# A fused attention and MLP kernel: another sequence for the same 883 operations

## The chip, the core and the metric

The kernel runs on one core of a Trainium2 chip. The core has engines that work side by side, each on its own queue and in order: PE (matrix products; PEld is its loading of weights), DVE and ACT and POOL (elementwise work), and SP, which here only issues DMAs. The metric is the device time in microseconds (us) of one execution. The profile is of one execution that the hardware profiler recorded.

## The reference, cut to what matters

```python
# S = 2048 rows, D = 448, F = 1792, 16 heads of 28; window of 8 keys, 2 apart
def A(x, wqkv, wo):                       # x is layernorm(input)
    q, k, v = split(x @ wqkv)             # 16 heads each
    idx = pos[:, None] - 2 * arange(8)    # below 0: masked
    attn = softmax(q . k[idx] * Dh ** -0.5)
    return (attn . v[idx]) @ wo
def B(x, w1, w2, w3, w4):                 # x is layernorm(h)
    g = gelu(layernorm(x) @ w1)           # four groups of 112 columns
    hs = [g0 down 1, g1 up 1, g2 down 2, g3 up 2] @ w2   # rows shifted, by group
    x1 = x + hs
    return x1 + gelu(layernorm(x1) @ w3) @ w4
h   = x + A(layernorm(x), wqkv, wo)
out = h + B(layernorm(h), w1, w2, w3, w4)
```

All inputs are bfloat16.

## The kernel before

**Tiles and stages.** The 2048 rows are 16 row tiles of 128. The first half of the work goes in four blocks of four row tiles (t = 0 to 3): N1 (first layernorm), A1 (q and k), V, A2 (logits and exp), A3 (attention times v, then wo and the residual), B1 (layernorm, w1, gelu). The second half goes in five units of 2, 4, 4, 4 and 2 row tiles (u = 0 to 4): B2 (w2 with the shifted groups, residual, statistics), T (layernorm and transposition), W3 (w3 and gelu) and B3 (w4, residual, output). Below, "W33" is stage W3 of unit 3, "T0" stage T of unit 0, and so on. Names of buffers: `lntm` holds normalized rows, `actT` the same transposed, `vt` and `vw` the values before and after they are laid out per window by DMAs, `bd_r` the attention weights spread into blocks by DVE (one of 16 products with the mask `bmask` each), `ht` the shifted rows of g that a DMA brings, `h3T` the gelu of w3's product, `qk_r` products and, at the end, output rows. `w3`, `w4`, and the two parts of w2 (`w2_s`, `w2_l`; `w_s` and `w_l` in the profile) are loaded by DMAs in pieces: w3 in two halves of 896 KB, w4 in two of 784 KB, `w2_l` in eight or so small pieces. The profile calls all of them `in_B_w_dram`, and their places in the arena `arena`.

**Rows turned.** A transposition of 128-column chunks is done by PE (matrix product with `ident`) or by a DMA (`DMA_TRANSPOSE actT<-lntm`), by block: `TURN` gives t or d for each.

**What sets the order.** The stages above are functions that only record operations, 883 in all, each with its engine, its instructions and the operations that it must follow. A table of numbers, `ORDER`, then lists all 883 in one sequence, and a second one, `OTHER`, names the operations that run on their second engine (an eviction of PE's results by DVE and not by ACT, or the other way round). `_Sched.arrange` walks through the sequence once and deals it out. Each engine gets its own operations in that order. Buffers (8 PSUM banks, 4 of `actT`, 2 of `bd_r`, 16 of `h3T` and so on) go to whoever comes next in the sequence, the longest free one first, and the new owner waits for the old one's last user. And DMA transpositions and plain DMAs of SP never overlap, as this piece of `arrange` (L207 to L212) says:

```python
            if op.insts[0][0] == "dma_start_transpose":
                op.deps.update(turned + moved)
                turned, moved = [op], []
            elif op.is_dma and not callable(op.chan):
                op.deps.update(turned)
                moved.append(op)
```

A transposition waits until every plain DMA listed since the last one has landed (`moved`), and plain DMAs wait until it has landed (`turned`); the stores of outputs, whose channel is a function, are free of both. So the place of a load in the table decides what the next transposition waits for.

All operations are emitted by one helper, so that the profile has nearly every instruction on line L1013 (waits that stand alone on L1011, ACT's table loads on L1008), and names of tiles tell the groups apart.

Of the kernel before, what the change touches and what calls it, by code (L numbers as in the profile page):

```python
# [17 lines left out]
RESIDUAL = 'ttvv'  # L18
DENSE = 2
ORDER = """  # L20
# [31 lines left out]
"""  # L52
OTHER = """
97 99 186 189 238 350 484 493 496 550 556
"""
FULL = (4,)
FILL = (0, 0, 0, 0)
# [997 lines left out]
```

## Time and profile before

| | |
|---|---|
| three runs | 191.86, 193.0, 195.99 us (median 193.0) |
| the profiled execution | 191.67 us, its span 190.0 us |
| granted TensorE clock, mean | 1.000 |
| PE busy | 181.8 us, 96% of the span, 2528 matmuls |
| DVE / ACT / POOL busy | 125.7 / 122.8 / 27.8 us |
| DMA queue q1 | 18.23 MB, 40.6% of 16 engines' span |

Busy shares are means over the span. The first 80 us hold the attention blocks, in which PE, DVE and ACT are all nearly always busy; after that DVE and ACT are busy a third to two thirds of the time and PE goes on.

### The profile page before, as it was taken

The numbers are of one execution on the slowest core, as the hardware profiler recorded it, in microseconds if no ns is written. First come the engines' busy times: TensorE is split into PE (matmuls) and PEld (weight loads), VectorE is DVE, ScalarE is ACT, GpSimd is POOL, SyncE is SP. The second block draws the span as 40 slices with busy tenths as digits, with TensorE's granted clock in tenths as the row PEclk, the third lists the DMA queues.
The fourth block names the chain that finished last, engine by engine and source line by source line (L and its number), as shares of the span: only waits on it lengthen the run. The fifth ranks groups of instructions, "written<-read, shape, count | busy, mean of one in ns | idle before, by whom it ended". The sixth has DMA issues, their size and how long they took to land.

```text
span 190.0 us, 5846 instructions
## 1 busy us (share of the span) xinstructions
PE 181.8 (96%) x2528; PEld 96.0 (51%) x2528; DVE 125.7 (66%) x220; ACT 122.8 (65%) x287; POOL 27.8 (15%) x67
## 2 busy tenths in 40 slices
PE   6999999998999999699999989999999999999994
PEld 2575335364534655475545534554445544455673
DVE  6989999999999899995378248823095357000503
ACT  3469999988999899675966878732715006630340
POOL 2380000000000000422260000060003507200000
PEclk9999999999999999999999999999999999999999
DMA  5990656853306599805033110571110600800401
GB/s 151 352 255 26 159 110 164 227 131 75 90 8 128 111 298 249 192 5 110 16 31 86 53 33 0 114 114 38 45 26 2 138 1 24 131 0 3 146 26 48
DMA packets 33634, 18.60 MB, mean 98 GB/s; under 512 B 21208, under 2 KB 33096, under 8 KB 33608
## 3 DMA queue, kind: packets, MB, share of 16 engines
q1 hardware_dynamic: 33608, 18.23, 40.6%
q8 instruction: 20, 0.33, 0.7%
q14 instruction: 6, 0.05, 0.1%
HBM read 8.14 MB, written 1.84 MB: 53 GB/s over the span
## 4 chain that ended last, share of the span: by engine, by line
PE 83%; DVE 5%; ACT 4%; DMA 3%; SPq 1%; issue 1%; POOL 1%; POOLq 0%; DVEq 0%
PE ps L1013 83%; ACT arena L1013 2%; DMA actT<-lntm 2%; SPq L1013 1%; DVE lntm L1013 1%; DVE arena L1013 1%; DMA w_l<-in_B_w_dram 1%; ACT actT L1013 1%; DVE st L1013 1%; DVE bd_r L1013 1%; DVE qk_r L1013 1%; POOL rs_y L1013 0%; ACT lntm L1013 0%; POOL ident L1013 0%; ACT h3T L1013 0%
## 5 line engine op out<-in xcount | busy, mean ns | idle before, releaser
L1013 PE MATMUL ps<-actT,arena 64*128 64x512 bf16 (+2 forms) x812 | 70.2, 325 | 2.4 <-DVE arena L1013 1.6
L1013 ACT ACTIVATE h3T<-ps 128x512 bf16<-128x512 f32 (+1 forms) x70 | 31.8, 513 | 41.5 <-PE ps L1013 41.0
L1013 PEld LDWEIGHTS ps<-actT,arena 64*128 64x128 bf16 (+1 forms) x812 | 35.6, 96 | 31.5 <-issue 3.4
L1013 PE MATMUL ps<-arena,h3T 64*128 64x448 bf16 (+3 forms) x434 | 44.3, 343 | 0.0
L1013 ACT ACTIVATE arena<-ps 128x512 bf16<-128x512 f32 (+6 forms) x67 | 30.8, 505 | 6.7 <-PE ps L1013 5.8
L1013 PEld LDWEIGHTS ps<-arena,h3T 64*128 64x128 bf16 (+1 forms) x434 | 22.6, 94 | 19.7 <-ACT h3T L1013 0.5
L1013 DVE TENSOR_TENSOR qk_r<-arena 128x4096 bf16<-128x4096 bf16 (+1 forms) x16 | 32.0, 2013 | 0.0
L1013 DVE SCALAR_TENSOR_TENSOR qk_r<-ps,mrs,arena 128x448 bf16<-128x448 f32 (+2 forms) x17 | 10.6, 652 | 30.2 <-PE ps L1013 30.2
L1013 POOL TENSOR_TENSOR arena<-arena,xin 128x448 f32<-128x448 f32 x16 | 16.5, 1056 | 78.6 <-ACT lntm L1013 61.6
L1013 DVE TENSOR_TENSOR bd_r<-arena,bmask 80x2048 bf16<-80x2048 bf16 x16 | 19.1, 1216 | 2.9 <-ACT arena L1013 2.9
L1013 DVE SCALAR_TENSOR_TENSOR arena<-xin,rs_y,ps 128x448 f32<-128x448 bf16 x16 | 10.4, 670 | 12.0 <-PE ps L1013 12.0
L1013 PE MATMUL ps<-wo_s,actT 64*128 64x448 bf16 x128 | 14.4, 350 | 0.1
L1013 PE MATMUL ps<-w_s,arena 64*128 64x448 bf16 x83 | 12.8, 350 | 0.8 <-DMA w_l<-in_B_w_dram 0.7
L1013 PE MATMUL ps<-arena,actT 64*128 64x448 bf16 x112 | 13.1, 350 | 0.2
L1013 PE MATMUL ps<-actT,w_s 64*112 64x512 bf16 x112 | 13.0, 378 | 0.0
L1013 ACT ACTIVATE actT<-ps 128x512 bf16<-128x512 f32 (+2 forms) x19 | 11.8, 643 | 0.6 <-PE ps L1013 0.6
L1013 ACT ACTIVATE lntm<-xin,nm 128x448 bf16<-128x448 bf16 x16 | 10.5, 665 | 1.7 <-DVE nm L1013 1.7
L1013 DVE TENSOR_SCALAR lntm<-arena,mv,rs_y 128x512 bf16<-128x512 f32 x14 | 8.2, 643 | 2.6 <-POOL rs_y L1013 2.0
L1013 DVE BATCH_NORM_STATS2 st<-xin 128x6 f32<-128x448 bf16 x16 | 9.2, 613 | 0.9 <-DMA xin<-in_A_x_dram 0.7
L1013 ACT ACTIVATE rs_x<-mv,epsilon 128x4 f32<-128x4 f32 (+2 forms) x16 | 4.7, 296 | 7.5 <-DVE mv L1013 7.2
L1013 PEld LDWEIGHTS ps<-actT,w_s 64*112 64x112 bf16 x112 | 7.1, 127 | 4.7 <-ACT arena L1013 0.5
L1013 PEld LDWEIGHTS ps<-w_s,arena 64*128 64x128 bf16 x83 | 5.4, 95 | 7.3 <-DMA w_l<-in_B_w_dram 1.1
(77 smaller groups left out, 165.3 us busy)
## 6 DMA issues: line engine op xcount, KB each, us to landing
arena<-in_B_w_dram SPq DMA_DIRECT2D x2, 896.0 KB, 6.3
out_dram<-qk_r SPq DMA_DIRECT2D x15, 112.0 KB, 1.8
arena<-in_B_w_dram SPq DMA_DIRECT2D x2, 784.0 KB, 9.2
vw<-vt SPq DMA_DIRECT2D x4, 320.0 KB, 6.0
vw<-vt SPq DMA_DIRECT2D x4, 256.0 KB, 4.6
arena<-in_A_wqkv_dram SPq DMA_DIRECT2D x2, 448.0 KB, 4.4
xin<-in_A_x_dram SPq DMA_DIRECT2D x2, 448.0 KB, 7.3
xin<-in_A_x_dram SPq DMA_DIRECT2D x3, 224.0 KB, 5.2
```

Of the source, the lines that this page charges most:

```text
L1013: inst = getattr(eng, meth)(**kw)
```

## The change

Only two tables of numbers change: `ORDER` gives another sequence of the same 883 operations, and `OTHER` another list. No function, no size and no buffer count changes, so all 2528 matmuls, all products of DVE, and all DMAs are the same ones. Of `ORDER`'s 23 lines none stays. The start, as a line or two show:

```diff
 ORDER = """
-0 5 6 8 1 9 44 45 2 7 55 56 57 60 46 47 48 10 65 38 41 67 29 61 49 58 66 62 63 68 69 70 50 51 52 53 54 59 92 64
+0 1 38 41 44 6 45 5 7 46 47 8 55 39 48 42 9 10 49 12 13 14 56 60 61 50 2 15 29 16 67 57 58 62 63 51 52 53 65 66
...
 OTHER = """
-97 99 186 189 238 350 484 493 496 550 556
+93 187 189 484 490 496 550 556
 """
```

What the new sequence does to the engines' queues is seen in their rows. Three places follow.

**PE, the first q and k.** PE's queue from the first transpositions of block 0 (the first row) on: `actT,arena 128x256` are q and k of block 0, `arena,actT 128x448` V of block 0, `ident,lntm 128x64` the transpositions of block 1, `64x256` the last columns of k and q of block 0, and 128x512 q and k of block 1. Before:

```order
L1013 MATMUL ps<-ident,lntm 128x128 x16
L1013 MATMUL ps<-actT,arena 128x256 x64
L1013 MATMUL ps<-arena,actT 128x448 x8
L1013 MATMUL ps<-actT,arena 128x256 x8
L1013 MATMUL ps<-arena,actT 128x448 x6
L1013 MATMUL ps<-ident,lntm 128x64 x32
L1013 MATMUL ps<-actT,arena 128x256 x12
L1013 MATMUL ps<-arena,actT 128x448 x14
L1013 MATMUL ps<-actT,arena 64x256 x16
L1013 MATMUL ps<-actT,arena 128x512 x8
```

Now:

```order
L1013 MATMUL ps<-ident,lntm 128x128 x16
L1013 MATMUL ps<-actT,arena 128x256 x60
L1013 MATMUL ps<-arena,actT 128x448 x8
L1013 MATMUL ps<-actT,arena 128x256 x24
L1013 MATMUL ps<-arena,actT 128x448 x8
L1013 MATMUL ps<-ident,lntm 128x64 x32
L1013 MATMUL ps<-arena,actT 128x448 x6
L1013 MATMUL ps<-actT,arena 64x256 x16
L1013 MATMUL ps<-arena,actT 128x448 x6
L1013 MATMUL ps<-actT,arena 64x256 x12
```

The 84 matmuls of q and k of block 0 stood in three pieces, the last of them behind the transpositions of block 1; now they are done before these, with 8 matmuls of V between.

**SP, the loads of w3 and w4.** SP's queue from the transposition for A1 of block 3 (the first row) past those for B1 of blocks 0 and 1 (the pair, x2) to the first half of w4. `in_B_w3_dram` is the second half of w3, `in_B_w4_dram` a half of w4; `vw<-vt` lays out values of blocks 2 and 3. Before:

```order
L1013 DMA_TRANSPOSE actT<-lntm 128x16x128
L1013 DMA vw<-vt 16x3x512
L1013 DMA vw<-vt 80x4x512
L1013 DMA vw<-vt 16x512 x2
L1013 DMA_TRANSPOSE actT<-lntm 128x16x128 x2
L1013 DMA vw<-vt 64x4x512
L1013 DMA arena<-in_B_w3_dram 128x2x1792
L1013 DMA w2_l<-in_B_w2_dram 64x448
L1013 DMA vw<-vt 64x4x512
L1013 DMA w2_l<-in_B_w2_dram 16x448
L1013 DMA w2_l<-in_B_w2_dram 48x448
L1013 DMA arena<-in_B_w4_dram 128x7x448
```

Behind them, before, stand `vw<-vt 80x4x512` and at once the second half of w4. Now:

```order
L1013 DMA_TRANSPOSE actT<-lntm 128x16x128
L1013 DMA arena<-in_B_w3_dram 128x2x1792
L1013 DMA vw<-vt 16x512
L1013 DMA vw<-vt 64x4x512
L1013 DMA w2_l<-in_B_w2_dram 16x448
L1013 DMA_TRANSPOSE actT<-lntm 128x16x128 x2
L1013 DMA w2_l<-in_B_w2_dram 48x448
L1013 DMA vw<-vt 80x4x512
L1013 DMA w2_l<-in_B_w2_dram 16x448
L1013 DMA vw<-vt 16x3x512
L1013 DMA w2_l<-in_B_w2_dram 48x448
L1013 DMA arena<-in_B_w4_dram 128x7x448
```

The second half of w3 stood behind the pair of transpositions (x2) and now stands ahead of it, right behind the transposition before. Between the halves of w4 stand three small loads now where one large one stood, and two of the large `vw<-vt` come behind the second half.

**SP, the shifted rows.** SP's queue at the middle of the kernel: `ht<-arena` brings the shifted rows of g for unit 2 (seven DMAs; before, the first of them stands ahead of the store), `w2_l` is a piece of w2's weights, the pair of transpositions are those for B1 of block 3 and for T2. Before:

```order
L1013 DMA out_0_dram<-qk_r 128x448
L1013 DMA ht<-arena 16x512
L1013 DMA ht<-arena 32x512
L1013 DMA ht<-arena 48x512 x2
L1013 DMA ht<-arena 64x512
L1013 DMA ht<-arena 16x512
L1013 DMA w2_l<-in_B_w2_dram 16x448
L1013 DMA_TRANSPOSE actT<-lntm 128x16x128 x2
```

Now:

```order
L1013 DMA_TRANSPOSE actT<-lntm 128x16x128
L1013 DMA ht<-arena 16x512 x2
L1013 DMA ht<-arena 48x512
L1013 DMA ht<-arena 32x512 x2
L1013 DMA ht<-arena 64x512
L1013 DMA ht<-arena 48x512
L1013 DMA_TRANSPOSE actT<-lntm 128x16x128 x2
```

The piece of `w2_l` is gone from behind the shifted rows (it is the `w2_l<-in_B_w2_dram 16x448` ahead of the pair of transpositions in the rows above), and the store of outputs no longer stands between the shifted rows.

60 rows, old and new, of the table ORDER are left out of this document.

## Prediction

> **What bounds the kernel now.** First the page: which engine is busy, and how much is missing.
>
> ```profile
> span 190.0 us, 5846 instructions
> PE 181.8 (96%) x2528; PEld 96.0 (51%) x2528; DVE 125.7 (66%) x220; ACT 122.8 (65%) x287; POOL 27.8 (15%) x67
> q8 instruction: 20, 0.33, 0.7%
> ```
>
> PE is busy for 181.8 of 190.0 us. No matmul is removed or added, so an order can win at most the other 8.2 us, less the head in which nothing has arrived and the tail in which only results leave. Second, the view by stretches of time says where those 8.2 us lie (stretch, its length, then busy time of PE, PEld, DVE, ACT, POOL with counts, clock, DMA share, GB/s):
>
> ```profile
> 0.00:8.00 8.00, 6.31 (x27) 2.58 (x27) 5.81 (x16) 3.75 (x10) 1.62 (x11) 1.00 0.72 229
> 35.00:46.00 11.00, 10.91 (x314) 6.02 (x310) 10.51 (x16) 10.19 (x26) 0.00 (x0) 1.00 0.64 161
> 46.00:60.00 14.00, 13.46 (x202) 6.11 (x198) 13.60 (x23) 13.27 (x37) 0.00 (x0) 1.00 0.32 69
> 60.00:76.00 16.00, 16.00 (x278) 8.97 (x278) 14.95 (x18) 15.22 (x34) 0.27 (x1) 1.00 0.80 202
> 76.00:79.00 3.00, 1.19 (x46) 0.64 (x47) 2.92 (x6) 2.41 (x4) 2.11 (x4) 1.00 1.05 240
> 105.00:113.00 8.00, 7.26 (x132) 3.40 (x128) 3.21 (x10) 6.43 (x14) 0.20 (x1) 1.00 0.19 51
> 160.00:165.30 5.30, 4.97 (x48) 2.07 (x44) 1.35 (x2) 3.54 (x8) 2.50 (x3) 1.00 0.69 105
> 165.30:190.00 24.70, 22.20 (x258) 14.02 (x258) 4.14 (x7) 6.38 (x18) 0.00 (x0) 1.00 0.14 46
> ```
>
> Length less PE's busy time is 1.69 at the head, 2.50 at the tail, and between them 0.54 (46 to 60), **1.81 (76 to 79)**, 0.74 (105 to 113) and 0.33 (160 to 165.3): 3.42 us. With head and tail that is 7.6 of the 8.2 us.  From 35 to 76 us DVE and ACT are nearly as full as PE, which matters for what can go wrong. Third, the timeline at each hole: the bracket is idle time ahead of the row and what ended it.
>
> ```profile
> 46.84 0.36 PE L1013 MATMUL ps<-xin,ident 64*128 64x448 bf16 x2 [0.54 <-issue]
> 78.98 0.39 PE L1013 MATMUL ps<-actT,arena 64*128 64x256 bf16 x3 [1.65 <-DVE arena L1013]
> 78.97 0.11 PEld L1013 LDWEIGHTS ps<-actT,arena 64*128 64x128 bf16 x4 [1.93 <-issue]
> 112.75 0.36 PE L1013 MATMUL ps<-w_s,arena 64*128 64x448 bf16 x1 [0.68 <-DMA w_l<-in_B_w_dram]
> 165.30 0.39 PE L1013 MATMUL ps<-actT,arena 64*128 64x256 bf16 x4 [0.33 <-DMA actT<-lntm]
> ```
>
> For the hole at 77 the matmul's row names DVE and the weight load's row names nothing ("issue"). I take the second. DVE's rows around it:
>
> ```profile
> 76.39 1.26 DVE L1013 SCALAR_TENSOR_TENSOR arena<-xin,rs_y,ps 128x448 f32<-128x448 bf16 x2
> 78.22 0.66 DVE L1013 SCALAR_TENSOR_TENSOR arena<-xin,rs_y,ps 128x448 f32<-128x448 bf16 x1
> ```
>
> By the sequence, the product that starts at 78.98 needs the bank that the first of the two evictions from 76.39 on gives back, which is done at about 77.1; the one that ends at 78.9 gives back another. What then holds PE? q8 moves instructions: 20 packets, 0.33 MB, so about 16 KB each, and by the counts, 2528 matmuls and as many weight loads over 20 packets, about 253 PE instructions each. Counted along PE's queue, the products that resume at 46.84 and at 78.98 are 1024 instructions apart, four times 256. So both holes sit at the same place within such a block, and I read them as PE waiting for its own next instructions. The view of the DMA queues from 75.5 to 79 us, and the loads issued ahead of it:
>
> ```profile
> q1 hardware_dynamic: 941, 0.83, 106.4%
> q8 instruction: 1, 0.02, 3.0%
> 65.39 0.61 SPq L1013 DMA_DIRECT2D arena<-in_B_w_dram  x1
> 69.09 0.77 SPq L1013 DMA_DIRECT2D arena<-in_B_w_dram  x1
> 69.91 0.75 SPq L1013 DMA_DIRECT2D vw<-vt  x1
> 70.70 0.61 SPq L1013 DMA_DIRECT2D arena<-in_B_w_dram  x1
> arena<-in_B_w_dram SPq DMA_DIRECT2D x2, 896.0 KB, 6.3
> arena<-in_B_w_dram SPq DMA_DIRECT2D x2, 784.0 KB, 9.2
> vw<-vt SPq DMA_DIRECT2D x4, 320.0 KB, 6.0
> ```
>
> One packet of q8 moves while q1 fills all engines (106.4%): the second half of w3, both halves of w4 and 320 KB of values were issued within 5.4 us, and a half of w4 takes 9.2 us to land (median). The instruction packet stands in that crowd.
>
> The Trainium skill, page "Runtime: NRT & Kernel Launch", section "Instruction fetch mechanics", says that instructions come in blocks of 16 KiB (256 instructions) over the sequencer's own DMA queue, and that crossing a boundary is mostly hidden. On the size the trace agrees (0.33 MB in 20 packets); on the hiding it speaks against my reading. By it the 1.93 us would be no fetch, the first term below 0, and the sum what the fourth rival gives.
>
> **The change part by part.** The sum starts from the profiled execution, 191.67 us.
>
> *The loads of w3 and w4 (SP).* The second half of w3 leaves the crowd: it now stands right behind the transposition for A1 of block 3, which is issued at 40.58 before.
>
> ```profile
> 40.58 1.96 SPq L1013 DMA_TRANSPOSE actT<-lntm  x1
> 46.68 1.27 SPq L1013 DMA_DIRECT2D vw<-vt  x2
> actT<-lntm SPq DMA_TRANSPOSE x10, 4.5
> ```
>
> By the median of 4.5 us to land, or by the 6.1 until the next plain DMA here, w3's half goes out at about 46 to 47.5 and not at 65.39. Behind the pair of transpositions, between 64.7 and 74 us, 896 KB fewer are issued, and the two large `vw<-vt` (576 KB) come behind the second half of w4 and not between or ahead. PE crosses the boundary at about 72 to 76 us either way, since its work up to there is the same. With the three big loads ahead of it the crossing cost 1.65 to 1.93; with two, and more spread, I take 0.3 left. Bounds: all of it goes (-1.9), or nothing (0), as w4's two halves of 9.2 us each are still there. **-1.5 us.** When that hole goes, the next thing late would be T0's transposed rows from DVE, which come up some 0.5 us earlier in its new queue.
>
> That half now flies near the boundary that PE crosses at 46 us, which cost 0.54 beside a transposition alone. Bounds: up to the price at 77 (+1.1), or a crossing behind the transposition (-0.5). I take 0, as the same transposition is the nearest row.
>
> *The piece of `w2_l` at 111 us.*
>
> ```profile
> 110.22 0.58 SPq L1013 DMA_DIRECT2D ht<-arena  x1
> 110.84 0.58 SPq L1013 DMA_DIRECT2D w_l<-in_B_w_dram  x1
> 110.84 1.87 DMA w_l<-in_B_w_dram
> ```
>
> (The last is a step of the chain that ended last, from issue to landing.) This load is the last of a row of eight, and PE waits 0.68 for it. Moved some 60 us ahead, it leaves the last `ht` as the last to land; that one was issued 0.62 earlier. A shifted row takes about as long as the piece of w2, and no store of outputs is issued among them now (another 0.6 us of SP). So PE's wait falls from 0.68 to about 0.1. Bounds: 0.68 gone, or 0.3 where an `ht` waits for the last gelu. **-0.6 us.**
>
> *The first q and k in one run.* PE starts the first q/k at 8.06, after warm-up, transpositions and ACT's evictions of these.
>
> ```profile
> 1.60 5.30 PE ps L1013 x15
> 6.92 1.09 ACT actT L1013 x2
> 8.06 3.67 PE L1013 MATMUL ps<-actT,arena 64*128 64x256 bf16 x64
> ```
>
> One of the four evictions of those transpositions goes to DVE now (`OTHER` gains 93), which stands beside ACT's; two on ACT in a row took 1.09, so up to 0.5 is won there, and I count 0.2. The order of q and k itself costs PE nothing: the same matmuls, and the switches between kinds of matmul are 53 for 52. What it shifts is when DVE's long products may start. DVE has 10.51 of 11.0 busy from 35 to 46, and the products of block 0 need all of q and k, which now come before block 1's transpositions. I take -0.5 in all up to T0, the bounds being -1.3 (of the 1.69 that PE isn't busy at the head all but 0.4) and +1.0.
>
> *T3 and T4.* Statistics of T4 stand in another order on DVE: a `qk_r` product of unit 2 that stood behind now stands ahead, but the first statistics come earlier by as much. Counted behind the start of W33, the transposition is issued at the same 5.9 us, and PE reaches it after the same 92 matmuls.
>
> ```profile
> 160.78 4.47 DMA actT<-lntm
> 154.87 10.09 PE L1013 MATMUL ps<-actT,arena 64*128 64x512 bf16 x92
> ```
>
> 0, with bounds -0.3 (the wait that is there) and +0.6 (one more product of DVE ahead).
>
> *ACT's tables.* Two more switches of table come with the new ACT order, among the gelus of W32.
>
> ```profile
> 109.39 1.28 ACT L1008 ACT_TABLE_LOAD   x1
> ```
>
> At 1.28 each that is 2.6 us of ACT, in a stretch in which it is busy for less than half. PE's products of B32 need the last gelu about 0.5 to 1 us after it is there by my count. I take 0; uncovered it is +2.6 at most. The Trainium skill, page "ScalarE: Activation LUTs", section "What ACT_TABLE_LOAD costs", counts a drain of about 1.4 us besides the load: by it the two would cost 5.3 us of ACT's time and some of that would show; the trace here has the load alone, 1.28 us.
>
> **Sum:** 191.67 - 1.5 - 0.6 - 0.5 = 189.1 on the scale of the profiled execution. The median of the three runs shown is 193.0, 1.3 above it, the lowest 191.86. I add 0.9, between them, and forecast **190.0 us**. What a measurement of this kernel can tell from no change is about 2%, here 189.1 to 196.9 around 193.0.
>
> **The rivals.**
>
> 1. *Instructions still come late.* The two halves of w4 are still issued within a few microseconds, and w3's half makes a second crowd at 46, so that the hole at 77 stays by half or the one at 46 grows. For it: w4's 9.2 us a half is the longest of the medians above. Against it: 896 KB less in the crowd. Of the 1.5 nothing is left: 190.6 profiled, with 0.5 more at 46 191.1, **192.0 us** run. Chance 0.20.
>
> 2. *All holes go.* Instructions come in time at both places, and the start gains its 1.3: 191.67 - 1.9 - 0.5 - 0.7 - 1.3 = 187.3, **188.2 us** run. For it: behind each hole stands PE work that waits for nothing. Against it: PE's crossings don't all fall on a quiet queue. Chance 0.14.
>
> 3. *Slower: the transposed rows of block 3 come too late.* Of block 1's values, 320 KB are laid out behind ACT's evictions of V at about 35.6 (counted along its queue), and behind w3's first half. They must land before block 3's transposition may go. I have it issued at 41.5 to 41.8 and landed at 46 to 48; the first product of A13, moved up on PE's queue, is due at about 47.7. What such a load took at worst, beside w4:
>
> ```profile
> vw<-vt SPq DMA_DIRECT2D x1, 320.0 KB, 9.1
> ```
>
> With that for the 6.0 of the median, the transposition goes 3.1 later; with 6.1 instead of 4.5 to land, 1.6 more. It decides from a landing later than 47.7 on: then PE stops, and DVE and ACT (13.60 and 13.27 of 14 us in the row from 46) have no room to catch up. 190.0 + 4.7 makes **194.7 us**, slower than before, and over 196.9 only if a second transposition is pushed off too. For it: the slack of 0 to 1.7 us. Against it: q1 is less than full there (0.64), so that a load need not take its worst. Chance 0.10.
>
> 4. *The holes are not instructions.* The wait at 78.98 is DVE's, as the matmul's row says; DVE's queue is as full as before and the hole stays. Then 191.67 - 0.6 - 0.5 = 190.6, **191.5 us** run. For it: that eviction ends 0.1 us ahead of PE's start. Against it: the bank, and the 1024 instructions between the two holes. Chance 0.12. This is the result that the section "Instruction fetch mechanics" of the Trainium skill would lead to.
>
> **How the numbers follow.** My case has 0.44, and by itself reaches from 188.9 to 191.2. For 8 in 10 the range holds it, rivals 1 and 4, half of rival 2 and half of rival 3: 187.9 to 194.0. Faster by over 2% (below 189.1) is rival 2 and a quarter of my case: 0.25. Slower (above 196.9) is less than half of rival 3: 0.04. The rest is 0.71.
>
> **What the profile after should show.** PEld's longest wait for "issue" below 0.6 us, none of 1.9; the second half of w3 issued at 46 to 48; the `w_l` row gone from PE's waits, and in its place at 112 us `ht` with at most 0.3; the first 128x256 matmul before 8.0; T4's wait 0.1 to 0.6; PE still 181 to 182 us busy; two more loads of ACT's tables, with no wait of PE behind them. I am wrong if a hole of over 1 us stands in the rows of PE between 40 and 60 us, if PE waits there for `actT<-lntm`, or if the hole at 72 to 79 us is as long as before with DMA below 0.9.

## The result, and the profile after

| | before | changed |
|---|---|---|
| median of four runs, us | 192.43 (191.69 to 195.99) | 189.43 (lowest 189.09) |
| ratio to before, 95% interval | 1 | 0.9858 (0.9817 to 0.9899) |
| an execution that was profiled, us | 191.67 | 189.02 |
| its span, us | 190.0 | 187.2 |

The change makes the kernel 1.4% faster, inside the 2% that were called no change, but clear of the runs' scatter. One of the changed kernel's four runs, the profiled one, took 234.95 us at a granted clock of 0.758 and is left out of the ratio; the trace read here is that of another execution, at clock 1.000, from the run a_same below (189.13 us median of six, ratio 0.9874, interval 0.9813 to 0.9935).

From the page of the changed kernel, busy times and the queue of instructions:

```profile
span 187.2 us, 5850 instructions
PE 181.2 (97%) x2528; PEld 96.1 (51%) x2528; DVE 123.4 (66%) x217; ACT 125.3 (67%) x292; POOL 27.3 (15%) x67
q8 instruction: 20, 0.33, 0.8%
```

PE's idle time fell from 8.2 to 6.0 us. The view by stretches, with the same bounds as before (stretch, length, busy time of PE, PEld, DVE, ACT and POOL with counts, clock, DMA share, GB/s), says where:

```profile
0.00:8.00 8.00, 5.76 (x27) 2.34 (x27) 5.93 (x16) 3.51 (x9) 2.08 (x14) 1.00 0.72 217
46.00:60.00 14.00, 14.00 (x214) 6.25 (x212) 13.97 (x23) 13.20 (x38) 0.00 (x0) 1.00 0.52 133
60.00:76.00 16.00, 15.68 (x267) 9.48 (x260) 14.83 (x17) 14.97 (x33) 0.27 (x1) 1.00 0.65 173
76.00:79.00 3.00, 2.88 (x84) 2.28 (x80) 2.89 (x5) 2.97 (x6) 0.82 (x2) 1.00 0.51 128
105.00:113.00 8.00, 7.59 (x76) 3.33 (x74) 3.61 (x12) 6.32 (x15) 0.20 (x1) 1.00 0.14 33
160.00:165.30 5.30, 5.30 (x62) 2.74 (x60) 0.00 (x0) 4.92 (x10) 0.94 (x1) 1.00 0.61 114
```

Idle from 46 to 60 is 0 (0.54 before), from 76 to 79 it is 0.12 (1.81), at 105 to 113 0.41 (0.74), before 165.3 0 (0.33). New is 0.32 between 60 and 76. The head has 0.55 more, but the warm-up alone is shorter by that (4.35 for 4.88), and the first q/k starts where it did (8.11 for 8.06). PE's rows in the timeline that still have a hole of 0.25 us or more after the warm-up:

```profile
6.41 1.42 PE L1013 MATMUL ps<-ident,lntm 128*128 128x128 bf16 x16 [0.46 <-DVE lntm L1013]
8.11 3.45 PE L1013 MATMUL ps<-actT,arena 64*128 64x256 bf16 x60 [0.29 <-DMA arena<-in_A_wqkv_dram]
66.02 2.58 PE L1013 MATMUL ps<-actT,w_s 64*112 64x512 bf16 x22 [0.32 <-DMA actT<-lntm]
110.47 0.36 PE L1013 MATMUL ps<-w_s,arena 64*128 64x448 bf16 x1 [0.27 <-DMA ht<-arena]
```

No row has "issue" behind its bracket any more; the weight loads' longest wait for it is now 0.4 us, of 1.9:

```profile
PEld ps L1013 <- issue: 8.1, 26, 0.4
```

### The profile page after: what moved, and what is told of

Same layout as the page of the kernel before. It is cut to its first block, busy times and chain, and to the rows that moved or that the text cites. A ratio compares the mean times of both kernels' runs of the same rounds, so it can differ in the third digit from the quotient of the medians.

```text
span 233.1 us, 5850 instructions
## 1 busy us (share of the span) xinstructions
PE 228.5 (98%) x2528; PEld 106.8 (46%) x2528; DVE 124.8 (54%) x217; ACT 127.1 (55%) x292; POOL 27.6 (12%) x67
## 4 chain that ended last, share of the span: by engine, by line
PE 96%; DMA 1%; DVE 1%; SPq 0%; issue 0%
PE ps L1013 96%; DMA xin<-in_A_x_dram 1%; DVE st L1013 0%; SPq L1013 0%; DVE qk_r L1013 0%; DVE lntm L1013 0%; DVE mv L1013 0%
## 5 line engine op out<-in xcount | busy, mean ns | idle before, releaser
L1013 PE MATMUL ps<-actT,arena 64*128 64x512 bf16 (+2 forms) x812 | 90.5, 387 | 0.3
L1013 PEld LDWEIGHTS ps<-actT,arena 64*128 64x128 bf16 (+1 forms) x812 | 39.0, 107 | 44.8 <-issue 27.8
L1013 PE MATMUL ps<-arena,h3T 64*128 64x448 bf16 (+3 forms) x434 | 57.8, 414 | 0.0
L1013 PEld LDWEIGHTS ps<-arena,h3T 64*128 64x128 bf16 (+1 forms) x434 | 25.9, 110 | 28.7 <-issue 0.9
L1013 PE MATMUL ps<-wo_s,actT 64*128 64x448 bf16 x128 | 18.1, 417 | 0.1
L1013 PE MATMUL ps<-actT,w_s 64*112 64x512 bf16 x112 | 16.8, 459 | 0.0
L1013 PE MATMUL ps<-arena,actT 64*128 64x448 bf16 x112 | 16.5, 415 | 0.1
L1013 PE MATMUL ps<-w_s,arena 64*128 64x448 bf16 x83 | 16.3, 419 | 0.1
L1013 PE MATMUL ps<-w_l,ht 64*128 64x448 bf16 x35 | 9.9, 419 | 0.0
L1013 PEld LDWEIGHTS ps<-wo_s,actT 64*128 64x128 bf16 x128 | 6.5, 105 | 7.4 <-issue 1.1
```

The costliest lines, as they stand in the source:

```text
L1013: inst = getattr(eng, meth)(**kw)
```

## The experiments

All of them are edits of the kernel before ("b_") or of the changed kernel ("a_"). A move is made on the list of numbers just before it is dealt out:

```diff
-        order = S.arrange([int(k) for k in ORDER.split()], ...)
+        seq = [int(k) for k in ORDER.split()]
+        seq.remove(28); seq.insert(seq.index(439) + 1, 28)      # which: see each run
+        order = S.arrange(seq, ...)
```

Numbers of operations: 28 second half of w3, 439 the transposition for A1 of block 3, 359 the third load of block 2's values (`vw`) behind it on SP's queue, 307 the transposition for B1 of block 1, 531 and 532 pieces of `w2_l`, 593 a store of outputs, 669 the last of the shifted rows (`ht`) of unit 2.

| run | edit | span | ratio to before, interval |
|---|---|---|---|
| a_same | none | 187.2 | 0.9874 (0.9813 to 0.9935) |
| b_shift | 14 narrow matmuls more in the warm-up | 191.6 | 1.0045 (0.9982 to 1.0107) |
| b_shift108 | 108 more | 189.4 | 0.9945 (0.9904 to 0.9985) |
| b_w3 | 28 behind 439 | 191.4 | 1.0021 (0.9982 to 1.0059) |
| b_w3_later | 28 behind 359 | 189.6 | 0.9965 (0.9931 to 0.9999) |
| b_w2l | 532 behind 531 | 189.9 | 1.0004 (0.9959 to 1.0048) |
| b_ht | 532 behind 531, 593 behind 669 | 189.1 | 0.9928 (0.9879 to 0.9976) |
| b_three | 28 behind 359, and b_ht | 188.0 | 0.9929 (0.9900 to 0.9959) |
| a_w3_back | 28 and 532 behind 307 | 190.0 | 0.9911 (0.9871 to 0.9951) |
| a_shift | 14 narrow matmuls more | 188.0 | 0.9826 (0.9788 to 0.9863) |

**a_same.** 

> The changed kernel once more, for a trace to read. My theory (late instructions, the late piece of w2, the start): span about 187.4 us, no idle of PE of over 0.6 us near 77 us, none before w_l near 112, the first 128x256 matmul before 8.0. Rival (the hole at 77 was DVE's and went because DVE's queue is ordered otherwise): the same span, but the place in PE's queue where instructions come in shows no wait in either kernel that depends on the DMA queue.

Span 187.2 as expected; the first 128x256 product is at 8.11 and not before 8.0.

**b_shift: are the holes instructions?** This edit makes PE's queue longer and moves nothing:

```diff
             for n in range(WARM):
-                keep_busy()
+                if n < WARM - 2:
+                    keep_busy()
+                else:
+                    mms([(busy(lambda v: v[:, 0:32]), ident[:], bass.AP(ident, 0, [[128, 128], [1, 32]]), True, True, 32, None)] * 8)
```

> The kernel before with the last two of the 11 warm-up matmuls cut into 8 narrow ones each (32 columns), so that PE's queue is 14 matmuls (28 instructions) longer ahead of all the work. Theory of late instructions in blocks of 256: both holes of PE move to products that stand 14 matmuls earlier in the program (some 2 to 4 us earlier, at 73 to 75 us and at 43 to 45 us). Rival (the holes are waits for DVE): they stay in front of the same products, at 77 and 46 us.

The two holes of its timeline:

```profile
47.08 0.41 PE L1016 MATMUL ps<-actT,arena 64*64 64x256 bf16 x6 [1.17 <-issue]
79.37 0.21 PE L1016 MATMUL ps<-bd_r,vw 80*32 80x64 bf16 x3 [1.37 <-issue]
```

They stand in front of other products: before, at `xin,ident` and at W30's `actT,arena` 64x256, the 720th and 1227th product of the work (warm-up not counted); now, at the 706th and the 1213th. Both moved by exactly 14, so by the 28 instructions put ahead. And the hole near 77 that the row before put down to DVE is put down to "issue" now. In time they hardly moved (the packets came at 44.88 and 76.17 us, for 44.64 and 75.83), which was expected wrong: 73 to 75 and 43 to 45.

**What a late packet is.** The trace has the time of each of q8's 20 packets. Call the place in PE's queue where a block of 256 instructions ends a crossing. There is one packet to each crossing, and where PE stands they read alike in every run: a packet is asked for at a crossing and needed at the next one, and PE goes on 1.3 to 1.6 us after the packet's end. (That it is asked for at the crossing is inferred from this. Where PE's products are long, the packet starts up to 2.2 us before the first product behind the crossing does.)

| run | crossing | packet of q8 | next crossing | hole | issued near the crossing |
|---|---|---|---|---|---|
| before | 42.20 | 44.64 to 45.56 | 46.84 | 0.54 | transposition 40.58 |
| before | 71.42 | 75.83 to 77.52 | 78.98 | 1.65 | w3 65.39, w4 69.09, 70.70 |
| a_same | 42.10 | 42.79 to 43.96 | 46.44 | 0 | transposition 42.24 |
| a_same | 46.44 | 46.60 to 47.86 | 53.08 | 0 | w3 47.02 |
| a_same | 72.07 | 74.43 to 75.40 | 77.21 | 0 | w4 69.14, 71.49 |
| b_w3 | 47.31 | 51.89 to 53.08 | 54.63 | 0.46 | w3 45.66 |
| b_w3_later | 46.82 | 48.86 to 50.08 | 53.55 | 0 | w3 47.26 |
| b_shift108 | 72.58 | 77.50 to 78.81 | 80.31 | 0.96 | w3 66.37, w4 69.85, 71.78 |
| a_shift | 71.86 | 74.05 to 75.19 | 76.69 | 0 | w4 69.61, 71.96 |

A hole is the delay of the packet, its own time and those 1.3 to 1.6 us, less PE's work in the block that it is in. Near 46 and 77 us these blocks hold 4 to 6 us of work, since they are of many small products; the others are mostly longer, and only a long delay shows behind them: 6.9 us of work did not hide a delay of 4.6 in b_w3, nor 6.8 us one of 4.9 in b_shift108.

The size of a hole differs between executions even where nothing was changed. b_w2l and b_ht below leave the order of all DMAs up to the second half of w4 as it was; their holes at 77 us are 1.17 and 0.90 where before had 1.65, and at 46 us 0.48 and 0.24 for 0.54. Each run has one trace, so a difference of this size between two runs shows nothing.

**b_shift108: the boundaries moved far.** The same edit with 9 groups of 13 for the last nine warm-up matmuls. 

> The kernel before, with nine of the 11 warm-up matmuls cut into 13 narrow ones each (32 columns): PE's queue is 108 matmuls longer ahead of the work, nothing else changes. By the trace of before PE then crosses its blocks of 256 instructions at about 38.7, 42.5, 47.3, 55, 65.2, 71.6 and 80.0 us, and no short block stands behind a crossing that falls into a transposition or right behind big loads. Theory of late instructions: both holes go, and the span falls by 1.5 to 2.2 us from 190.0, less what the narrow matmuls cost at the start (0 to 1.3). Rival (the order of the work decides): holes as before, span 190 to 191.

```profile
6.73 0.40 PE L1016 MATMUL ps<-ident,lntm 128*128 128x128 bf16 x4 [0.99 <-DVE lntm L1016]
80.31 0.94 PE L1016 MATMUL ps<-actT,arena 64*128 64x256 bf16 x14 [0.96 <-issue]
```

The hole at 46 is gone and that at 77 with it, but one of 0.96 stands at the next boundary, 80.31: its crossing (72.58) fell behind all three big loads, where a packet is late by 4.9 us. 0.6% are won with no operation moved. I had expected none to be left.

**b_w3: one load of the change alone.** 

> The kernel before with one load moved: the second half of w3 goes right behind the transposition for A1 of block 3. Theory of late instructions: the hole of 1.65 us of PE at 77 us shrinks to 0.3 or so and the time falls by 1.2 to 1.9 us, unless the hole at 46 grows by as much as 1. Rival (the hole is DVE's): the hole stays, time as before within 0.4 us.

```profile
54.63 0.39 PE L1015 MATMUL ps<-actT,arena 64*128 64x512 bf16 x2 [0.46 <-issue]
79.13 0.61 PE L1015 MATMUL ps<-actT,arena 64*128 64x256 bf16 x8 [0.70 <-DVE arena L1015]
113.99 0.36 PE L1015 MATMUL ps<-w_s,arena 64*128 64x448 bf16 x1 [1.13 <-DMA w_l<-in_B_w_dram]
```

The hole at 77 is 0.70, not the 0.3 expected, and below the 0.90 of b_ht, which leaves w3's half in its place, by no more than executions differ. And 0.46 comes up at 54.63 where there was none: issued at 45.66, the load stood in front of the packet of the crossing at 47.31. Another hole of 0.30 stands at 42.98, ahead of the moved load. Together with a longer wait for `w_l` nothing is won (1.0021).

**b_w3_later: the same load, 1.6 us later.** 

> The kernel before with the second half of w3 moved ahead, as in the run b_w3, but issued behind three small and large loads of values, at about 48.5 us and so behind PE's crossing at 47 instead of 1.5 us ahead of it. Theory: the packet of that crossing is no longer late (it was 4.6 us late in b_w3), the hole of 0.46 at 54.6 goes, the one at 77 stays at 0.7 or so as in b_w3; time 0.7 to 1.2 us below before. Rival: what counts is only how many bytes are moved in all of 46 to 56 us; holes as in b_w3, time as before.

```profile
78.24 0.50 PE L1015 MATMUL ps<-actT,arena 64*128 64x256 bf16 x6 [0.90 <-DVE arena L1015]
```

The load goes out at 47.26, 0.4 us after the crossing. The packet is late by 2.0 and not 4.6, the hole at 54 is gone, the one at 77 is 0.90; time 0.35% below before (interval 0.01 to 0.69%), at the lower end of what was expected. For the hole at 54, then, it isn't the bytes of this stretch that count but which of the two, load or crossing, comes first; this rests on one trace of each run.

**a_w3_back: the load put back in the changed kernel.** 

> The changed kernel with the second half of w3 (and the piece of w2_l that must follow it) moved back behind the pair of transpositions, to 66 us, as before. Theory (late instructions behind a crowd of loads): the packet for the crossing at 72 us comes 1 to 2 us later than its 74.43, the hole at 77 us is back with 0.5 to 1.9 us, time longer by as much. Rival (w3's place doesn't matter, the hole went by another place of the blocks or of w4's loads): no hole, time within 0.3 us.

```profile
73.53 0.42 PE L1016 MATMUL ps<-bd_r,vw 80*32 80x64 bf16 x32 [1.50 <-ACT rs_y L1016]
66.62 0.39 SPq L1016 DMA_DIRECT2D arena<-in_B_w_dram  x1
68.03 0.65 SPq L1016 DMA_DIRECT2D vw<-vt  x1
69.37 0.62 SPq L1016 DMA_DIRECT2D vw<-vt  x1
vw<-vt SPq DMA_DIRECT2D x2, 48.0 KB, 5.6
vw<-vt SPq DMA_DIRECT2D x2, 320.0 KB, 6.0
```

(The last two rows are DMA issues from 64 to 76 us, KB and median us to landing.) The span of the profiled execution is 2.8 us longer, but by the ratios only 0.4% is lost, and their intervals overlap (0.9871 to 0.9951, and 0.9813 to 0.9935), so that a loss is not settled. There is no hole at 77: on this the rival was right and the theory wrong. The hole of 1.50 is in front of a product that reads the laid-out values `vw`, two loads of which now stand behind w3's half. The one issued at 68.03 landed at 73.44 by the trace, 0.09 us before the product. The row names ACT, whose instruction ended at the same time (73.37); that it is the load is read from these times, not shown by a run of its own. PE's crossing then came at 74.43, and its packet was late by 2.2 only. Neither theory had the late values: in the new sequence w3's early place may also be what lets them come in time.

**b_w2l and b_ht: the wait at 112.** 

> The kernel before with one load moved: the last piece of w2_l goes from behind the shifted rows (111 us) to behind another piece of w2_l (74 us). Theory: PE's wait of 0.68 us at 112 falls to 0.1, time less by 0.5 to 0.7 us. Rival (the shifted rows themselves are late): less by under 0.2 us.

> The kernel before with the last piece of w2_l moved ahead as in the run b_w2l, and also the store of outputs that stands among the shifted rows moved behind them. Theory (SP issues one DMA each 0.6 us, and the last of the row decides): PE's wait at 112, 0.68 before and 0.48 in b_w2l, falls to 0 to 0.2. Rival (the last gelu decides when the row of shifted rows can go on): it stays at 0.3 to 0.5.

First b_w2l's row, then those of b_ht:

```profile
112.34 0.36 PE L1015 MATMUL ps<-w_s,arena 64*128 64x448 bf16 x1 [0.48 <-DMA ht<-arena]
```

```profile
105.20 5.20 SPq L1016 DMA_DIRECT2D ht<-arena  x7
110.44 0.59 SPq L1016 DMA_DIRECT2D out_dram<-qk_r  x1
111.86 0.35 PE L1016 MATMUL ps<-w_s,arena 64*128 64x448 bf16 x1
```

Without the piece of `w2_l` PE still waits 0.48, for the last `ht`; without the store as well it waits not at all. Of the 0.68, the piece of w2 was 0.2 and the store the rest, in these executions (the same wait was 0.84 in b_w3_later and 1.13 in b_w3, which leave these DMAs alone). In b_w2l the gain was lost at T4's transposition (wait 0.67 for 0.33 before). That the time falls by 0.7% in b_ht is more than this wait is worth; its trace has smaller holes at 46 and 77 us too.

**b_three: do they add up?** 

> The kernel before with the three moves of the runs b_w3_later and b_ht in one: the second half of w3 behind the values of block 2 at about 48 us, the last piece of w2_l ahead, the store behind the shifted rows. If the terms add up: the hole at 77 at 0.7 to 0.9, the wait at 112 at 0 to 0.1, time 1.2 to 1.6 us below before, so half of what the new sequence wins. If they don't (what is won early is lost at the next wait): 0.5 to 0.8 below.

```profile
46.80 0.36 PE L1017 MATMUL ps<-xin,ident 64*128 64x448 bf16 x2 [0.48 <-issue]
77.65 1.05 PE L1017 MATMUL ps<-actT,arena 64*128 64x256 bf16 x16 [0.37 <-DVE arena L1017]
```

The time falls by 0.7% (1.4 us), as expected if they add up; span 188.0, the hole at 77 was 0.37 in this execution, and at 112 no row has a wait of 0.25 or more. But b_ht alone gave as much (0.9928; here 0.9929), and the two parts together would give 1.1%. So that w3's move adds anything to b_ht is not shown. Three moved operations in the old sequence give about half of the new one's gain by the ratios, and two of them (b_ht) as much.

**a_shift: is the new sequence free of holes by chance?** 

> The changed kernel with the last two warm-up matmuls cut into 8 narrow ones each, as in the run b_shift: PE's queue 14 matmuls longer ahead of the work. By the trace of the changed kernel the crossings come at 42.0, 45.5, 52.0, 71.4 and 76.2 us; at 42.0 the packet still goes ahead of the transposition (42.24). Theory: the packet asked for at 71.4 lands at 75 to 75.5 beside w4, 1.4 us before PE can use it, so that PE stands for 0.2 to 0.8 us in front of the product that is the 1213th of the work, at 76 to 77 us; none at 46; time longer by as much. Rival (the new order is free of such holes wherever its blocks end): no hole, time as the changed kernel's.

No hole at 76, time as the changed kernel's. The packet ended at 75.19, and PE came to the boundary at 76.69, 1.5 us later, which is just what it needs (1.3 to 1.6 in the holes seen). So the expectation failed by a few tenths, and how much room the new sequence has isn't settled.

## Why the prediction was right

The forecast was 190.0, measured 189.4 and 189.1; on the scale of the profiled execution the sum said 189.1 and the execution took 189.02. That it is met to 0.1 us is luck: the terms were not all right, and their errors cancel.

| term | predicted | by the two traces | |
|---|---|---|---|
| hole at 77 | -1.5 | -1.69 | size right; late instructions by b_shift, but what freed them not shown |
| hole at 46 | 0 | -0.54 | failed |
| `w2_l` at 111 | -0.6 | -0.33 | too large |
| start and all up to T0 | -0.5 | +0.05 and +0.32 | failed |
| T4 | 0 | -0.33 | at its bound of -0.3 |
| ACT's tables | 0 | 0 | right |

- **Late instructions.** The reading "issue" against "DVE" held. The first reason given for the gain, "896 KB less in the crowd", did not. At the crossing near 72 us the packet was late by 4.41, 4.22 and 4.05 us in the old sequence with w3's half in that crowd (before, b_w2l, b_ht; 3.23 and 4.92 with the crossing shifted, in b_shift and b_shift108), by 4.12, 4.22 and 3.80 with it away (b_w3, b_w3_later, b_three), and by 2.36, 2.19 and 2.23 in the new one (a_same, a_shift, a_w3_back), in the last of these with it put back. So the delay goes with something else in the new sequence. The prediction's other reason, that the two large `vw<-vt` come behind the second half of w4, fits all eleven; no run moved these alone, so the cause of the shorter delay stays open. PE's block there holds less work now (5.1 us for 5.9), so only the shorter delay saves it, and a_shift's packet came with nothing to spare.
- **The place beside a crossing.** What the new sequence has besides is the place of loads beside PE's crossings: the transposition goes out 0.14 us behind one (it was 1.6 ahead), w3's half 0.6 behind the next. In SP's rows of the changed kernel:

```profile
42.24 3.04 SPq L1013 DMA_TRANSPOSE actT<-lntm  x1
47.02 0.39 SPq L1013 DMA_DIRECT2D arena<-in_B_w_dram  x1
```

- **46 us.** The step that failed was "the same transposition is the nearest row": the transposition is the same, its issue moved from 40.58 to 42.24, past the crossing at 42.1. The prediction had it at 41.5 to 41.8 and did not set that against the crossing. In the seven traces of the old sequence with a crossing at 42.2 to 43.2 us, right behind this transposition's issue, the packet is late by 1.9 to 2.4 us; in the three of the new one, where the crossing comes first, by 0.7 to 0.9.
- **`w2_l`.** The step named two causes, the piece of w2 and the store, and took their sum to be nearly 0.68, which b_ht shows. In the changed kernel 0.27 was left; what held the last `ht` there was not tried.
- **The start.** The step took ACT's evictions for what holds the first q/k. In the changed kernel the row names a load, and the chain that ended last has it right ahead of PE:

```profile
2.70 5.16 DMA arena<-in_A_wqkv_dram
8.11 9.99 PE ps L1013 x180
```

  So an earlier eviction wins nothing. And the next thing late was to be T0's transposed rows; PE ran into the transposition for B1 instead (0.32 at 66.02): with the holes gone, DVE's products and that transposition are the next to bound this stretch, and the chain leaves PE there:

```profile
45.82 1.22 DVE bd_r L1013
47.04 2.20 DVE qk_r L1013
49.33 4.39 DVE qk_r L1013 x2
59.99 5.90 DMA actT<-lntm
66.02 4.00 PE ps L1013 x36
```

- **T4.** The reorder of its statistics was counted as even, with a wait of 0.1 to 0.6 to be seen; PE had no wait there. Which of the moved rows did it was not tried.
- **Rival 3** (block 3's rows too late) did not come: the transposition went out at 42.24, 0.4 to 0.7 later than counted, and A13 did not wait. Rival 4 is excluded by b_shift, rival 1 by the trace. Of rival 2 the half on the holes came, both gone, and the half on the start did not, which is why its 188.2 was not reached. The Trainium skill, page "Runtime: NRT & Kernel Launch", section "Instruction fetch mechanics", has such crossings mostly hidden: the trace of before agrees for 18 of its 20 packets, and not for those that PE needs at 46.84 (0.54 us) and 78.98 (1.65 us).

## What to carry to other kernels

When PE idles and the weight load's row says "issue", count PE's instructions between the holes; a multiple of 256 points to its own instructions coming late, and a few narrow matmuls ahead of the work, which shift every boundary, show whether it is so. In a stretch of many small products, try big loads and DMA transpositions just behind PE's crossing into the next 256 instructions, not just ahead of it. Judge a moved load by all that it passes on its queue: here w3's half alone won nothing, 1.6 us later 0.35%, and put back into the new sequence it stood ahead of values that then came late. And before a smaller hole is put down to a move, look at the same hole in runs that leave it alone: here it went from 0.90 to 1.65 by itself.

## What the runs showed of the hardware

PE had one block of 256 instructions in hand: a packet of 16 KB asked for at a crossing was needed at the next one in every hole seen, and PE went on 1.3 to 1.6 us after its end. The packet took 0.9 to 1.8 us itself. It waited up to 4.9 us (b_shift108) where loads of 784 to 896 KB had been issued ahead of it, and 2.4 us (before, 42.2 to 44.64) where only a DMA transposition had. That transposition kept the engines as full as the loads did (96.9% in b_shift108 from 72.6 to 77.5 us), and no packet of q8 moved meanwhile:

```profile
q1 hardware_dynamic: 1788, 0.45, 97.0%
```

The packet moved from 44.64 on, as the transposition's traffic ran out (from 44 to 47 us q1 has 11.9% of the engines' time). Where the crossing came first, the same transposition held the packet less: in b_shift108 the crossing is at 44.23, the transposition's first packets move at 44.71, and that of q8 starts at 45.60. A full q1 does not set the delay by itself: in a_same it was at 106.4% from 72.1 to 74.4 us, and the packet was late by 2.4 only.
